# A second layer in f16 halves instead of fp32r, one attention chunk back to f16, more tiles and a new written order

## The chip, the cores and the metric

One NeuronCore of a Trainium2 chip runs the whole program. The metric is the device time of one execution in microseconds, taken as the median of several runs. Its compute engines are TensorE (PE in the profile: matmuls; PEld: the loading of their stationary operand), VectorE (DVE) and ScalarE (ACT). SyncE (SP) issues all data transfers here. GpSimd (POOL) only clears a few tiles at the start.

## The reference, cut to what matters

An attention with a complex decaying state is followed by a two-layer network. Batch is 4, heads 8, sequence 768, head width 48; the network is 384 to 2048 to 384 over 3072 rows.

```
scale = min(mag, 0.999) / (mag + 1e-6)          # mag = |a_re + i a_im|
for t in range(S):
    S_re, S_im = (a * S).re + k_t v_t^T, (a * S).im      # a = scaled a_re + i a_im
    y[t] = q_t @ S_re
x = y as rows of 384                             # 4 * 768 rows
h = x @ w_in
out = (h - tanh(h)) @ w_out
```

## The kernel before, in words

The sequence is cut into six chunks of 128 positions. A unit u is one chunk of one batch entry, so u runs from 0 to 23, chunk u // 4. A group g is two units, 256 rows of the network, and there are NG = 12 groups.

**The gates** (`gates_b` to `gates_e`, letters B, b, C, D, E in the written order) turn a_re and a_im of a group into decay factors and angles: logarithms, exponentials, an arctan, a cumulative sum over the 128 positions as a matmul with a triangle of ones (`cumsum`, L224 in fp32 for the first groups, L227 in f16 after them), sines. ScalarE must load a table of functions when it changes between logarithm, arctan or tanh, and sine.

**The products** (`products`, letter p) scale q and k of a unit with these factors (L395, L398: tile qkf) and bring them into transposed form, in fp32 through TensorE for the first chunk ("plain"), later split into a high and a low f16 part and transposed by a transfer that SP issues (L410, tiles qT and kT). The products of a unit also split v (tile vv, L421 and L422).

**The attention** (`attention`, letter a) forms the scores from kT and qT, masks them (tile af or a16), adds what the carried state z gives to q (L471), multiplies the masked scores with v (y, L478 in fp32, L481 in f16), writes the unit's rows as f16 halves x16, transposes them by a transfer into xT (L493), and updates the state z with k and v. A product of two split operands is three matmuls, high by high, high by low and low by high (`PASS`). For units below WIDE = 8, that is chunks 0 and 1, y and the state update take fp32 operands, without a split: one fp32 matmul per head, which the profile records as two. Units below PLAIN = 4 also have fp32 scores.

**The weights** come as 64-bit floats. `decode` (letters i and o for tile numbers of the first and second layer) loads a tile of 128 by 384 and builds the 32-bit value from the halves with three operations of VectorE (L187, L191, L192) and one of ScalarE (L110). Then ScalarE writes a high part and VectorE the low part. First-layer tiles become f16 pairs; second-layer tiles become fp32r pairs, a 4-byte format of TensorE. There are 16 tiles of each kind. The loaded tile is an io tile (three of them) or, for some, a borrowed mg tile; the scratch is a wtmp tile (three) or a borrowed mt tile, as the strings ROOM say.

**The network** works on a group at a time, in eight steps fp of two hidden tiles. `head` runs 18 f16 matmuls (L529) into a PSUM tile h (three of them), then tanh on ScalarE into an mt tile (two) and h - tanh(h) on VectorE over it. `split` writes the fp32r high part on ScalarE and the low part on VectorE into an mg tile (three). `tail` runs 12 matmuls of 384 columns (L554) into two PSUM tiles that collect all eight steps; it is written LAG = 4 steps behind the head. After step 7 ScalarE copies the sums out to an io tile and SP stores them.

**What sets the order.** START, FIRST, SECOND and CYCLE are lists written by hand: START is what comes ahead of the first group, FIRST and SECOND what is woven between the steps of groups 0 and 1, CYCLE that of all later ones. "8:a2" means: at place 8 (step 4, before its split) one more part of the attention of unit 2g + 2. On top of that each kind of operation has a priority offset (EARLY for groups 0 and 1, OFFSET later), by which the scheduler puts the instructions of each engine in order. Each engine and SP then run their queues in that order. So chunk 1, units 4 to 7, is worked on within groups 1 and 2.

**The guards.** Sums of squares and similar numbers of many tiles are collected in `stats`; `check_stats` compares them with limits and sets a flag. If the flag is set, a slow general version (`tile_general`) runs; it isn't set here. The check stands ahead of the last group's steps.

Of the kernel before, what the change touches and what calls it, by code (L numbers as in the profile page):

```python
# [84 lines left out]
def tile_fast(ctx: ExitStack, tc: tile.TileContext, flag, a_in, qkv_in, win_in, wout_in, sq_c, vec_c, lim_c, out):  # L85
# [84 lines left out]
    def decode(ft, kinds=(0, 1)):  # L170
        for kind in kinds:
            src = (win_in, wout_in)[kind]
            n = len(wi) + len(wo)
# [5 lines left out]
            SP("dec").dma_start(out=raw, in_=src[:, ft].bitcast(I32).rearrange("p (n two) -> p n two", two=2))
            if ROOM["wtmp"][n] == "1":  # L180
                tmp = sb.tile([P, 512], F32, name="mt", bufs=2)[:, :DM].bitcast(I32)
            else:
                tmp = sb.tile([P, DM], I32, name="wtmp", bufs=3)
# [248 lines left out]
    def attention(u):  # L432
# [3 lines left out]
        if g not in xTs:  # L436
            xTs[g] = sb.tile([P, 2, 2, KT, P], F16, name="xT", bufs=2)
# [392 lines left out]
```

## Time and profile before

| what | us |
|---|---|
| median of three runs | 596.84 |
| the three runs | 596.11, 596.84, 601.57 |
| the profiled execution | 599.23 |
| its span | 597.4 |
| TensorE matmuls busy | 532.2 |
| TensorE weight loads busy | 478.5 |
| VectorE busy | 469.1 |
| ScalarE busy | 465.2 |

The profile is of one execution, a little slower than the median. Its lines read: source line, engine, operation, the tile written and the tiles read, the shapes, and the count; then busy time, the mean of one in nanoseconds, and how long the engine idled just before, with what ended that. L100 is the line of a helper through which most operations are issued, so these are told apart by their tiles. A timeline line is the start, the length and the instructions, merged where they follow each other. Matmuls overlap, so a record is longer than the spacing of two of them. A wait "X <- Y" names the engine that idled and the operation whose end released it. The granted clock is the share of full speed that TensorE was given.

### The profile page before, as it was taken

To read this page: it belongs to the slowest core of one execution; us is meant where nothing else is said; L and a number is where in the kernel's file an instruction comes from. 1 tells how busy PE (TensorE), PEld (TensorE's weight loads), DVE (VectorE), ACT (ScalarE), POOL (GpSimd) and SP (SyncE) were. 2 spreads that over 40 slices of the span, in tenths; PEclk is the share of its full clock that TensorE was granted. 3 is DMA by queue.
4 is the path that set the end of the run, shared out by engine and by line. 5 is a ranking of instruction groups with operands and counts; after the bars stand their busy time and mean duration, and the time that the engine had idled before them with its cause. 6 is when DMAs were issued, how large, how long until landed. Compare 5 with 4: busy or idle time off the path is not lost.

```text
span 597.4 us, 12550 instructions
## 1 busy us (share of the span) xinstructions
PE 532.2 (89%) x4994; PEld 478.5 (80%) x4994; DVE 469.1 (79%) x790; ACT 465.2 (78%) x905; POOL 2.1 (0%) x8
## 2 busy tenths in 40 slices
PE   2464795988999999998999999999999999999995
PEld 0253694987998998997998998989989989999994
DVE  5887899678798498898898998988988988854330
ACT  7979697598897497888998998988989979553331
POOL 1000000000000000000000000000000000000000
PEclk9868798799999699999999999999999999999998
DMA  7738516317566287176275294593573652710001
GB/s 259 216 124 232 166 54 176 94 51 144 132 122 153 54 159 154 58 126 164 53 145 133 55 192 110 76 168 100 105 157 68 132 104 55 140 55 14 22 7 31
DMA packets 133901, 68.07 MB, mean 114 GB/s; under 512 B 119982, under 2 KB 123694, under 8 KB 133836
## 3 DMA queue, kind: packets, MB, share of 16 engines
q1 hardware_dynamic: 133836, 67.21, 49.7%
q8 instruction: 40, 0.66, 0.4%
q14 instruction: 25, 0.20, 0.1%
HBM read 36.73 MB, written 4.78 MB: 69 GB/s over the span
## 4 chain that ended last, share of the span: by engine, by line
PE 50%; ACT 26%; DVE 9%; DMA 8%; issue 4%; SPq 0%; ACTq 0%; DVEq 0%
PE o L554 18%; PE h L529 16%; PE att L100 10%; ACT a_raw L100 4%; ACT L100 4%; DMA kT<-k 3%; ACT mg L100 3%; DMA qT<-q 3%; ACT junk L100 3%; ACT mt L100 3%; PE att L478 2%; PE att L471 2%; ACT g_t L100 2%; PE att L227 2%; ACT q L100 2%
## 5 line engine op out<-in xcount | busy, mean ns | idle before, releaser
L554 PE MATMUL o<-wo,mg 128*128 128x384 f32 x1152 | 226.8, 345 | 2.7 <-ACT mg L100 2.3
L529 PE MATMUL h<-xT,wi 128*128 128x256 f16 x1728 | 210.0, 275 | 3.1 <-DMA xT<-x 3.0
L554 PEld LDWEIGHTS o<-wo,mg 128*128 128x128 f32 x1152 | 196.2, 189 | 4.9 <-ACT mg L100 2.9
L529 PEld LDWEIGHTS <-wi 128*128 128x128 f16 x1728 | 164.5, 99 | 34.2 <-issue 10.3
L100 DVE TENSOR_TENSOR mg<-mt,mg 128x512 fp32r<-128x512 f32 x96 | 65.8, 687 | 37.4 <-ACT mg L100 37.2
L100 DVE SCALAR_TENSOR_TENSOR mt<-h,mt 128x512 f32<-128x512 f32 x96 | 65.4, 687 | 27.2 <-ACT mt L100 26.6
L100 ACT ACTIVATE mt<-h 128x512 f32<-128x512 f32 x96 | 55.8, 589 | 38.6 <-PE h L529 27.7
L100 ACT ACTIVATE mg<-mt 128x512 fp32r<-128x512 f32 x96 | 59.8, 625 | 25.5 <-PE o L554 25.3
L100 ACT ACT_TABLE_LOAD x39 | 50.0, 1283 | 1.3 <-PEq L823 0.8
L100 PE MATMUL att<-qT,kT 96*128 96x128 f16 (+1 forms) x544 | 44.2, 235 | 3.7 <-DMA kT<-k 3.0
L100 ACT ACTIVATE a_raw<-a_raw 128x768 f32<-128x768 f32 (+2 forms) x49 | 39.0, 797 | 0.2 <-DVE a_raw L100 0.2
L398 DVE TENSOR_TENSOR qkf<-qkv_raw,g_trig 128x768 f32<-128x768 f32 x40 | 37.3, 950 | 0.0
L100 PEld LDWEIGHTS <-kT 96*128 96x128 f16 x480 | 29.0, 99 | 7.5 <-DMA kT<-k 3.9
L100 DVE SCALAR_TENSOR_TENSOR g_t<-g_t,a_raw 128x768 f32<-128x768 f32 (+1 forms) x26 | 23.1, 890 | 0.5 <-ACT a_raw L100 0.5
L100 PE MATMUL att<-sqc,qkf 128*96 128x128 f32 x32 | 6.6, 370 | 18.6 <-DVE qkf L398 18.6
L100 DVE TENSOR_TENSOR af<-att,sqc 128x512 f32<-128x512 f32 x32 | 21.9, 686 | 1.3 <-PE att L100 0.4
L100 ACT ACTIVATE a<-af 128x512 f16<-128x512 f32 x32 | 19.2, 626 | 4.0 <-DVE af L100 4.0
L100 DVE TENSOR_TENSOR a<-af,a 128x512 f16<-128x512 f32 x32 | 21.2, 682 | 1.0 <-ACT a L100 0.9
L100 ACT ACTIVATE g_trig<-g_t 128x768 f32<-128x768 f32 (+1 forms) x26 | 20.3, 786 | 1.8 <-DVE g_t L100 1.7
L100 PEld LDWEIGHTS att<-sqc,qkf 128*96 128x96 f32 x32 | 4.8, 169 | 20.7 <-DVE qkf L398 11.7
L117 DVE TENSOR_TENSOR q<-qkf,q 128x768 f16<-128x768 f32 x20 | 19.0, 952 | 2.2 <-ACT q L100 2.2
L100 ACT ACTIVATE q<-qkf 128x768 f16<-128x768 f32 x20 | 16.8, 842 | 4.0 <-DMA qT<-q 3.9
(102 smaller groups left out, 732.9 us busy)
## 6 DMA issues: line engine op xcount, KB each, us to landing
qkv_raw<-in_qkv SPq DMA_DIRECT2D x24, 576.0 KB
a_raw<-in_a SPq DMA_DIRECT2D x22, 384.0 KB
io<-in_wout SPq DMA_DIRECT2D x15, 384.0 KB
io<-in_win SPq DMA_DIRECT2D x14, 384.0 KB
out_dram<-io SPq DMA_DIRECT2D x24, 192.0 KB
a_raw<-in_a SPq DMA_DIRECT2D x4, 192.0 KB
mg<-in_win SPq DMA_DIRECT2D x2, 384.0 KB
mg<-in_wout SPq DMA_DIRECT2D x1, 384.0 KB
```

The costliest lines, as they stand in the source:

```text
L100: return f(*a, **k)
L117: by_name[ENGINE[which]](kind).tensor_tensor(**k)
L227: T("cum").matmul(c_ps[:, :HD], lhsT=tri, rhs=hl[:, bb, i], start=(i == 0), stop=(i == 1))
L398: V("prod").tensor_tensor(out=f, in0=x[:, :, None].broadcast_to([P, H, 2, D]), in1=tg[:, :, sl].rearrange("p r (h d) -> p h r d", d=D), op ...
L471: T("qu").matmul(u_ps[:, h * D:(h + 1) * D], lhsT=qT[0:K, qp * H + h], rhs=z16[0:K, zp, h * D:(h + 1) * D], start=(h == 0 and n == 0), sto ...
L478: T("y").matmul(y_ps[:, h * D:(h + 1) * D], lhsT=a16[h // 4][:, (h % 4) * P:(h % 4 + 1) * P], rhs=vv[0][:, h * D:(h + 1) * D], start=(h == ...
L529: T("h").matmul(h_ps[:, j].rearrange("p (two t) -> p two t", two=2), lhsT=wi[ft][:, wp, kt * P:(kt + 1) * P], rhs=xT[:, :, xp, kt, :], sta ...
L554: T("o").matmul(o_ps[tt][:, :DM], lhsT=gg[:, gp, j * 256 + tt * P:j * 256 + (tt + 1) * P], rhs=wo[ft][:, wp], start=(ft == 0 and n == 0), ...
```

## The change

- Both kinds of weight tile are f16 pairs, with the same scale. The split of h - tanh(h) goes to f16, with a factor 2 to the 15; the low part is made by a scalar_tensor_tensor instead of a tensor_tensor. The copy of the sums out takes the factors away again.
- WIDE goes from 8 to 4: in chunk 1 too, v, the masked scores and k are split to f16, and y and the state update are three f16 matmuls per head.
- Tiles (BUFS): io and wtmp 4 instead of 3 and without borrowing, mt 4 instead of 2, mg 5 instead of 3 (each half as large), qT 3 instead of 2; the others stay.
- New guards: the copy of the sums out of all groups but the last collects its sum ("o", 22 of them), and the last group squares its eight high parts ("g"). The check moves from ahead of the last group to behind its steps, before the last tails.
- The lists START, FIRST, SECOND and CYCLE and the priority offsets are new. The engines of all operations stay.

```diff
-WIDE = 8
-ROOM = {"io": "00000000000000000000110000010000", "wtmp": "11001011101001010000000000000000"}
+WIDE = 4
+BUFS = {"io": 4, "wtmp": 4, "mt": 4, "mg": 5, "qkf": 2, "xT": 2, "a16": 3, "af": 2, "xf": 1, "x16": 1, "qT": 3, "kT": 2, "vv": 2, "z16": 2}
 START = (
-    "o0 F0 o7 q0 F1 B1 b1 i1 p0 p0 q1 p1 i3 i0 p1 i5 p1 p0 o3 i2 a0 a0 o1 i6 i8 a1 i7 o4 a0 E1 a0 o5 a1 a1 i11 a1 o6 C1 i10 o2 D1 i4 a0 "
+    "q0 i3 F0 F1 i1 o7 p0 q1 B1 p1 i5 o3 i0 p0 p1 b1 p1 p0 a0 a0 o1 a1 a1 i7 E1 o4 a0 i8 a0 i6 i2 i10 i11 a1 o5 a1 C1 o2 i15 a0 o6 i4 D1 "
 ).split()
...
 CYCLE = tuple((int(i), x) for i, x in (y.split(":") for y in (
-    "0:p2 0:w0 1:p2 2:p3 2:p3 2:p2 5:C2 5:D2 5:a2 5:a2 6:p3 6:a3 7:a2 7:a2 8:a3 9:a3 10:B3 10:a2 10:a3 10:a3 11:E2 11:b3 12:w1 14:a2 "
+    "0:p2 1:p2 2:p3 3:p3 4:w0 4:p2 5:C2 5:p3 5:D2 5:a2 5:a2 6:a3 7:a2 7:a2 8:a3 9:a3 10:B3 10:a2 10:a3 10:a3 11:E2 11:b3 13:a2 15:w1 "
 ).split()))
...
-            if kind == 0:
-                t = wi[ft] = const.tile([P, 2, DM], F16, name=f"wi{ft}")
-            else:
-                t = wo[ft] = const.tile([P, 2, DM], F32R, name=f"wo{ft}")
+            t = const.tile([P, 2, DM], F16, name=f"w{kind}_{ft}")
+            (wi, wo)[kind][ft] = t
...
-        th = sb.tile([P, 512], F32, name="mt", bufs=2)
+        th = sb.tile([P, 512], F32, name="mt", bufs=BUFS["mt"])
...
-        gg = sb.tile([P, 2, 512], F32R, name="mg", bufs=3)
-        copy("ghi", "ghi", gg[:, 0], th)
-        combine("glo", "glo", out=gg[:, 1], in0=th, in1=gg[:, 0], op=ALU.subtract)
+        gg = sb.tile([P, 2, 512], F16, name="mg", bufs=BUFS["mg"])
+        copy("ghi", "ghi", gg[:, 0], th, 2.0 ** SG)
+        V("glo").scalar_tensor_tensor(out=gg[:, 1], in0=th, scalar=2.0 ** SG, in1=gg[:, 0], op0=ALU.mult, op1=ALU.subtract)
+        if g == NG - 1:
+            A("guard").activation(out=junk()[:, :512], in_=gg[:, 0], func=AF.Square, accum_out=stat("g"))
...
-                copy("out", "out", o_sb[:, tt], o_ps[tt][:, :DM])
+                A("out").activation(out=o_sb[:, tt], in_=o_ps[tt][:, :DM], func=AF.Copy, scale=2.0 ** -(SG + SW), **({"accum_out": stat("o")} if g < NG - 1 else {}))
...
-        if g == NG - 1:
-            check_stats()
...
+    check_stats()
     for x in pend:
         tail(*x)
```

Of the priority offsets, those of the later groups change so (a lower one lets others pass ahead): tanh from 700 to -2000, the masked scores (af) from 4000 to -300, the state's high part (zhi) from 2000 to 100, v's low part (vlo) from 0 to 1000, the transfers in (load) from 2000 to 400, the weights' (dechi, declo) from 30 and -300 to 100 and 200, mt from 200 to 400; a few others by less.

More of the change, by code (lines that the diff above doesn't have):

```diff
@@ L59 @@
-ENGINE = {"qhi": "A", "khi": "A", "qlo": "V", "klo": "V", "cos": "V", "sin": "V", "zhi": "A", "qux": "A", "zmul": "V", "out": "A", "xf0": "A", "tr": "A", "vd": "A", "lsb0": "V", "lsb1": "V", "base": "A", "dechi": "A", "declo": "V", "abs": "A", "thhi": "A", "t2hi": "A", "t2lo": "V", "xhi": "A", "xlo": "V", "vhi": "A", "ahi": "A", "alo": "V", "ghi": "A", "glo": "V", "nf": "A", "t1": "V"}
+OFFSET = {"gate": 2000, "gatep": 700, "prod": 0, "prodp": -100, "qkhi": -30, "vhi": -30, "vlo": 1000, "zhi": 100, "zlo": -300, "S": 30, "af": -300, "ahi": -30, "alo": -2000, "qu": 0, "y": 0, "xf": -30, "kv": 2000, "z": 100, "guard": -2000, "h": 0, "tanh": -2000, "mt": 400, "ghi": 2000, "glo": -30, "o": 0, "out": -100, "dec": -100, "dechi": 100, "declo": 200, "table": -30, "cum": 0, "load": 400}
@@ new lines @@
+EARLY = {"gate": 2000, "gatep": 100, "prod": 0, "prodp": 0, "qkhi": -30, "vhi": 0, "vlo": -2000, "zhi": 1000, "zlo": -300, "S": 100, "af": 1000, "ahi": -700, "alo": -30, "qu": 0, "y": 4000, "xf": 0, "kv": 700, "z": 200, "guard": -700, "h": 0, "tanh": 30, "mt": 400, "ghi": 100, "glo": 30, "o": 0, "out": 700, "dec": 0, "dechi": 1000, "declo": 4000, "table": -300, "cum": 0, "load": 0}
+ENGINE = {"qhi": "A", "khi": "A", "qlo": "V", "klo": "V", "cos": "V", "sin": "V", "zhi": "A", "qux": "A", "zmul": "V", "xf0": "A", "tr": "A", "vd": "A", "lsb0": "V", "lsb1": "V", "base": "A", "dechi": "A", "declo": "V", "abs": "A", "thhi": "A", "t2hi": "A", "t2lo": "V", "xhi": "A", "xlo": "V", "vhi": "A", "ahi": "A", "alo": "V", "ghi": "A", "glo": "V", "nf": "A", "t1": "V"}
@@ L172, in decode @@
             src = (win_in, wout_in)[kind]
-            n = len(wi) + len(wo)
-            if ROOM["io"][n] == "1":
-                raw = sb.tile([P, 2, 512], F32R, name="mg", bufs=3).rearrange("p two n -> p (two n)")[:, :2 * DM]
-            else:
-                raw = sb.tile([P, 2, DM], F32, name="io", bufs=3).rearrange("p two n -> p (two n)")
-            raw = raw.bitcast(I32).rearrange("p (n two) -> p n two", two=2)
+            raw = sb.tile([P, 2, DM], F32, name="io", bufs=BUFS["io"]).rearrange("p two n -> p (two n)").bitcast(I32).rearrange("p (n two) -> p n two", two=2)
             SP("dec").dma_start(out=raw, in_=src[:, ft].bitcast(I32).rearrange("p (n two) -> p n two", two=2))
[L180 to L183, printed above, removed]
+            tmp = sb.tile([P, DM], I32, name="wtmp", bufs=BUFS["wtmp"])
             lo, hi = raw[:, :, 0], raw[:, :, 1]
@@ L202, in weight_stats @@
         A("guard").activation(out=junk()[:, :DM], in_=wi[ft][:, 0], func=AF.Square, accum_out=stat("w"))
-        A("guard").activation(out=junk()[:, :DM], in_=wo[ft][:, 0], func=AF.Square, scale=2.0 ** 10, accum_out=stat("w"))
+        A("guard").activation(out=junk()[:, :DM], in_=wo[ft][:, 0], func=AF.Square, accum_out=stat("w"))
     gate = {}
@@ L395, in products @@
             V("prod").scalar_tensor_tensor(out=x, in0=vw(e), scalar=E_MAX, in1=x, op0=ALU.min, op1=ALU.mult)
-            f = kf if wide and i else sb.tile([P, H, 2, D], F32, name="qkf", bufs=2)
+            f = kf if wide and i else sb.tile([P, H, 2, D], F32, name="qkf", bufs=BUFS["qkf"])
             n = "qk"[i]
@@ L436, in attention @@
         if g not in xTs:
[L437 removed]
+            xTs[g] = sb.tile([P, 2, 2, KT, P], F16, name="xT", bufs=BUFS["xT"])
         xT = xTs[g]
@@ L441, in attention @@
         if c > 0:
-            z16 = sb.tile([P, 2, HD], F16, name="z16", bufs=2)
+            z16 = sb.tile([P, 2, HD], F16, name="z16", bufs=BUFS["z16"])
             zs = float(2.0 ** (SU - SZ))
@@ L460, in attention @@
                 continue
-            ah = sb.tile([P, 2, 512], F16, name="a16", bufs=3)
+            ah = sb.tile([P, 2, 512], F16, name="a16", bufs=BUFS["a16"])
             a16.append((ah, af))
@@ L487, in attention @@
         else:
-            xf = sb.tile([P, HD], F32, name="xf")
+            xf = sb.tile([P, HD], F32, name="xf", bufs=BUFS["xf"])
             copy("xf0", "xf", xf, y_ps[:, :HD], xs)
-        x16 = sb.tile([P, 2, HD], F16, name="x16")
+        x16 = sb.tile([P, 2, HD], F16, name="x16", bufs=BUFS["x16"])
         copy("xhi", "xf", x16[:, 0], xf)
```

37 lines of the change are left out of this document (18 added, 19 removed).

## The prediction

> **What bounds the kernel now.** First the page's busy times, then the busy times by stretch. I cut the span where TensorE starts the first-layer matmuls of a new group of 256 rows: the first at 64.25 us, the second at 128.42, the fourth at 219.92; 361.27 to 402.68 is one whole later group, and from 520.58 on no attention is left to prepare. The columns are the length, then PE, PEld, DVE, ACT and POOL busy (with instructions), granted clock, DMA share and GB/s.
>
> ```profile
> PE 532.2 (89%) x4994; PEld 478.5 (80%) x4994; DVE 469.1 (79%) x790; ACT 465.2 (78%) x905; POOL 2.1 (0%) x8
> ```
>
> ```profile
> 0.00:64.25 64.25, 27.95 (x137) 20.50 (x138) 49.28 (x104) 54.14 (x114) 2.08 (x8) 0.82 0.68 202
> 64.25:128.42 64.17, 54.99 (x373) 48.70 (x372) 53.29 (x104) 48.80 (x91) 0.00 (x0) 0.86 0.40 117
> 128.42:219.92 91.50, 87.73 (x780) 79.53 (x781) 71.32 (x111) 74.03 (x142) 0.00 (x0) 0.94 0.57 116
> 361.27:402.68 41.41, 40.50 (x441) 36.84 (x441) 37.30 (x61) 37.18 (x74) 0.00 (x0) 1.00 0.61 116
> 520.58:597.40 76.82, 69.41 (x592) 64.06 (x589) 28.45 (x46) 25.88 (x47) 0.00 (x0) 0.98 0.11 29
> ```
>
> The reader is to see four regimes. Up to 128.4 us TensorE waits for the others, which decode weights. In groups 1 and 2 (128.42 to 219.92) it is busy 87.7 of 91.5 us, partly at a lower clock. In the nine groups from 219.92 on it is the bound: 40.50 of 41.41 us, with VectorE and ScalarE close behind (37.30 and 37.18, 90%). At the end it runs alone. So a shorter TensorE instruction pays in full from 219.92 on, and only while the other two stay below it. The waits (total, times, longest) say what is late elsewhere:
>
> ```profile
> PE att L100 <- DVE qkf L398: 18.6, 3, 8.4
> PE att L227 <- ACT a_raw L100: 8.1, 8, 2.6
> ```
>
> **Second layer in f16 (term 1).** 1152 matmuls at L554 keep their count and their 384 columns. Their spacing is read from runs without a gap: the difference of a long and a short run of one kind. The same width in f16 is in the trace too, the cumulative sums of L227. Rows: start, length, what. The grouped lines and the counts by stretch follow.
>
> ```profile
> 163.75 0.49 PE L227 MATMUL att<-g_t,tri 128*128 128x384 f16 x2
> ...
> 462.10 0.82 PE L227 MATMUL att<-g_t,tri 128*128 128x384 f16 x4
> ...
> 575.15 2.33 PE L554 MATMUL o<-wo,mg 128*128 128x384 f32 x12
> ...
> 579.22 10.65 PE L554 MATMUL o<-wo,mg 128*128 128x384 f32 x60
> ```
>
> ```profile
> L554 PE MATMUL o<-wo,mg 128*128 128x384 f32 x1152 | 226.8, 345 | 2.7 <-ACT mg L100 2.3 <-DVE mg L100 0.4
> ...
> L227 PE MATMUL att<-g_t,tri 128*128 128x384 f16 x40 | 8.5, 328 | 0.0
> ```
>
> ```profile
> 128.42:219.92 91.50, 32.23 (x156) 27.29 (x156) 0.94 0.57 116
> 219.92:597.40 377.48, 178.37 (x913) 154.55 (x912) 1.00 0.47 98
> ```
>
> Now (10.65 - 2.33) / 48 = 173.3 ns; f16 (0.82 - 0.49) / 2 = 165 ns. The saving is 8.3 ns each: 913 x 8.3 = 7.6 us after 219.92, and 1.3 us for the 156 in groups 1 and 2, which belongs to term 3. Bounds: nothing, if the 173 ns come from the tile and not from the type; and 17 ns by the two means (345 - 328), 15.5 us. I take **-7.6**, since a spacing counts and not a length.
>
> The Trainium skill speaks against this term: "FP8 and Floating Point Precision", section TensorE Precision Notes, lists four passes for true FP32 and has reduced-precision FP32 merely read 4 bytes and cut them. By that, both forms are one pass over the same columns and term 1 is 0. The 173.3 against 165 ns above disagree, on two rounded rows.
>
> What feeds these matmuls does not change in price by any row: the high part stays a ScalarE copy (f32 to f16 is among the forms below at 626 ns), the low part becomes a scalar_tensor_tensor in place of a tensor_tensor, and the factors ride along. By the rows under term 3 the one form costs 682/512 = 1.33 ns a column and the other 550/384 = 1.43; were it 0.1 ns dearer, that is 0.4 us of VectorE a group (8 x 512 columns), beside TensorE's 40. I take 0.
>
> **More tiles for tanh and its split (term 2).** In each late group TensorE stops once, before the cumulative sum of L227, for ScalarE:
>
> ```profile
> 395.79 2.14 PE L529 MATMUL h<-xT,wi 128*128 128x256 f16 x18
> ...
> 398.62 0.60 ACT L100 ACTIVATE mt<-h 128x512 f32<-128x512 f32 x1 [1.36 <-DVE mg L100]
> ...
> 402.68 0.48 PE L227 MATMUL att<-a_raw,tri 128*128 128x384 f16 x2 [0.90 <-ACT a_raw L100]
> ```
>
> The tanh at 398.62 waits for one of two mt tiles, which the low-part operation frees. Its matmuls ended at 397.93, so 0.7 us of the 1.36 are the tile's. The arctan that TensorE waits for stands behind it in ScalarE's queue. With four mt tiles the 0.90 us stop can shrink to 0.2; what is late next is the table load and the copy of the angle. Eight stops of 0.7 are 5.6 us; at best all 8.1 us of the wait above go. I take half, **-3**, since tanh's priority also falls (from 700 to -2000); the bad end of that is worked out as a rival.
>
> The Trainium skill, "Perfetto Trace Analysis", section Optimization Strategy, reads a repeated bubble on the engine that should be full as a possible lack of tile space. By that rule the whole 8.1 us would go with the new tiles; the rows above give the tile only 0.7 of the 0.9 us.
>
> **Chunk 1 back to f16 (term 3).** Units 4 to 7 (attention of chunk 1, run in groups 1 and 2) get 24 f16 matmuls for y and 24 for the state update, where 16 records each stand now (8 fp32 matmuls are 16 records). Spacing is the start of the next row less the start:
>
> ```profile
> 149.06 1.96 PE L478 MATMUL att<-qkv_raw,a 128*128 128x48 f32 x16
> 150.86 0.82 PE L529 MATMUL h<-xT,wi 128*128 128x256 f16 x6
> ...
> 164.74 1.48 PE L100 MATMUL att<-af,vv 128*96 128x48 f32 x16
> 166.05 1.25 PE L529 MATMUL h<-xT,wi 128*128 128x256 f16 x10
> ...
> 449.57 0.78 PE L471 MATMUL att<-z,qT 96*128 96x48 f16 x24
> 450.19 0.56 PE L481 MATMUL att<-vv,a 128*128 128x48 f16 x16
> ```
>
> y 1.80 to 0.62, state 1.31 to 0.62 (24 matmuls of the same 48 columns): 1.87 us per unit, 7.5 us of TensorE for four. Against it stands work on the other two engines:
>
> ```profile
> L100 DVE TENSOR_TENSOR a<-af,a 128x512 f16<-128x512 f32 x32 | 21.2, 682 | 1.0 <-ACT a L100 0.9
> ...
> L100 ACT ACTIVATE a<-af 128x512 f16<-128x512 f32 x32 | 19.2, 626 | 4.0 <-DVE af L100 4.0
> ...
> L421 DVE SCALAR_TENSOR_TENSOR vv<-qkv_raw,vv 128x384 f16<-128x384 f32 x16 | 8.8, 550 | 1.0 <-ACT vv L100 1.0
> ...
> L100 ACT ACTIVATE vv<-qkv_raw 128x384 f16<-128x384 f32 x16 | 8.3, 521 | 0.1
> ...
> L422 DVE TENSOR_SCALAR vv<-vv,vec 128x768 f16<-128x768 f16 x16 | 6.6, 412 | 0.1
> ...
> L110 ACT ACTIVATE af<-qkv_raw,vec 128x384 f32<-128x384 f32 x6 | 3.5, 603 | 0.2 <-PE att L100 0.2
> ```
>
> VectorE: 2 x 682 + 550 + 412 = 2.33 us per unit, 9.3 in all. ScalarE: 2 x 626 + 521 - 603 = 1.17, 4.7 in all. In the 91.5 us VectorE goes from 71.3 to 80.6 and ScalarE from 74.0 to 78.7, TensorE from 87.7 to 78.9. These groups then hold the same work as a late one, which takes 41.41 - 0.8 (96 x 8.3 ns) = 40.6 us: two take 81.2, 10.3 less than now. The loads of the raw q, k, v also move, from behind the y matmuls to the end of the products, four of them, each earlier on SP's queue; SP waits for y there now:
>
> ```profile
> SPq L152 <- PE att L478: 13.8, 4, 6.5
> ```
>
> Bounds: -10.3, and +9.3 if all of VectorE's new work falls on the path. These groups still start late and cold after group 0, so I take half the good end, **-5**.
>
> **New order and tiles at the start (term 4).** Up to the first group the lists hold the same 19 weight tiles, six product steps and nine attention steps; only their order differs, and the decode's scratch is four io and four wtmp tiles instead of three and three with loans from mg and mt. The transposes of the first q and k wait for VectorE:
>
> ```profile
> 35.44 1.91 PE L100 MATMUL att<-sqc,qkf 128*96 128x128 f32 x8 [8.42 <-DVE qkf L398]
> ...
> SPq L179 <- DVE wtmp L192: 35.0, 12, 9.3
> ```
>
> While TensorE waits there, VectorE does decode work. The new list puts q0, p0 and p1 ahead of most tiles, and a fourth io tile loosens SP's 35 us of waits for a free one, behind which the attention's transfers queue. But VectorE and ScalarE are busy 102.6 and 102.9 of the first 128.4 us, and that work stays. Bounds: all 18.6 us of waits for qkf above, or one wait more of 8.4. Nearest to nothing: **-2**.
>
> **Guards and the end (0).** 22 output copies get a read of the accumulator (0.2 us each, as the row below), 0.4 us of ScalarE a group, beside TensorE's 40. Eight squares of 512 columns in the last group, at most 0.63 + 0.20 us each, lie where ScalarE is busy 25.9 of 76.8 us. The check comes behind the last of them instead of ahead of the last group; its load of limits then stands on SP ahead of nothing but the last outputs, and only the flag waits for it.
>
> ```profile
> L100 ACT ACTIVATION_READ_ACCUMULATOR junk<-xf 128x1 f32 x24 | 4.7, 194 | 0.0
> ```
>
> ```profile
> 590.02 0.15 DVE L100 TENSOR_SCALAR flag<-att 1x1 int32<-1x1 f32 x1 [5.00 <-PE att L100]
> ```
>
> ```profile
> L778 SPq EVENT_SEMAPHORE  x8: 17/17/17, 595.5 to 596.0; - x8
> L778 SPq COMPARE_BRANCH  x1: 53/53/53, 591.6 to 591.6; - x1
> ```
>
> The branch on the flag is done at 591.6; the end waits for the outputs to land, to 595.5. A flag up to 3.9 us later costs nothing; without that cover the last square and its read (0.8 us) would be added.
>
> **Sum.** The profiled execution took 599.23 us (span 597.4 and 1.8 around it): 599.2 - 7.6 - 3 - 5 - 2 = 581.6. The median shown, 596.84, is 2.4 lower, so **579.2**.
>
> **The rivals.**
> (a) The second layer does not get faster (term 1 at its bound of nothing): 579.2 + 7.6 = **586.8**. For it: the f16 spacing rests on short runs of one fixed weight tile. Against it: the two spacings differ by 8 ns. The Trainium skill's rule quoted under term 1 gives this result too.
> (b) VectorE and ScalarE become the bound in the late groups. They are at 90% with 41.41 us; at 40.6 ScalarE with its reads stands at 37.6, 93%, in strict order on each engine. If the period stays, terms 1 and 2 go but for the last stretch (592 records, some 190 of them second layer, 1.6 us): 579.2 + 6.0 + 3 = 588.2, and half of term 3 with it, **590.7**. Against it: the stops of TensorE in a late group are 0.9 us.
> (c) Slower: the splits of chunk 1 stand between the scores and y. In each of units 4 to 7 TensorE would wait for two high and two low parts, 2 x (0.626 + 0.682) = 2.6 us, and lose its clock as it does now after its wait for a transposed k:
>
> ```profile
> 193.00:206.00 13.00, 13.00 (x122) 11.94 (x118) 6.32 (x12) 4.15 (x10) 0.00 (x0) 0.61 0.27 76
> ```
>
> 13 us at 0.61 lose 5.1. Four times 7.7 is 30.8, less the 7.5 that the matmuls save: +23.3 in place of -5, 579.2 + 28.3 = **607.5**. It decides from 5.0 us lost per unit on: 4 x 5.0 - 7.5 is +12.5 in place of -5, as much as the forecast gains. Against it: from 219.92 on the same splits leave the clock at 1.00.
> (d) The order at the start gives most of the waits for qkf, 14 instead of 2: **567.2**.
>
> **How the numbers follow.** Forecast 0.50 (own range 571 to 587), (a) 0.09, (b) 0.17, (c) 0.12, (d) 0.12. A measurement of this kernel tells about 1%, 6 us, from no change: faster means below 590.9, slower above 602.8. Forecast, (a), (d) and a third of (b): 0.77 faster; the rest of (b) 0.11 the same; (c) 0.12 slower. The range runs from (d) to where (c) begins, 565 to 602.
>
> **What would show it.** Right: runs of 60 second-layer matmuls near 9.9 us; late groups of 40 to 40.6 us with TensorE stopped under 0.5 us; groups 1 and 2 together near 86; the first first-layer matmul within 3 us of 64. Wrong: 173 ns kept (a); late groups still at 41.4 with ScalarE or VectorE at the waits' head (b); a clock below 0.9 in the y matmuls of chunk 1 (c); first layer starting before 55 (d).

## The result and the profile after

| | before | after |
|---|---|---|
| median, us (four runs each, same chip) | 596.53 | 575.27 |
| range of the runs | 596.11 to 601.57 | 574.78 to 577.2 |
| the profiled execution | 599.23 | 575.09 |
| its span | 597.4 | 573.3 |

The ratio is 0.9631 [0.9575, 0.9687]: faster by 3.7%. The forecast was 579.2.

First the busy times on the page of the kernel after, then its busy times by stretch, cut at the same places as before: where TensorE starts the first-layer matmuls of group 0, 1, 3 and 11. The columns are the length, PE, PEld, DVE, ACT and POOL busy (with instructions), granted clock, DMA share and GB/s.

```profile
PE 502.8 (88%) x5058; PEld 385.8 (67%) x5058; DVE 475.2 (83%) x806; ACT 474.1 (83%) x951; POOL 2.3 (0%) x8
```

```profile
0.00:68.25 68.25, 26.81 (x128) 18.49 (x129) 55.33 (x119) 56.66 (x121) 2.26 (x8) 0.91 0.71 212
68.25:116.44 48.19, 46.50 (x369) 37.86 (x370) 45.96 (x90) 42.01 (x80) 0.00 (x0) 0.95 0.44 124
116.44:209.18 92.74, 79.55 (x863) 59.50 (x861) 80.97 (x131) 83.75 (x161) 0.00 (x0) 0.98 0.58 113
209.18:527.27 318.09, 310.51 (x3411) 241.75 (x3412) 279.76 (x450) 273.96 (x554) 0.00 (x0) 0.99 0.53 114
527.27:573.30 46.03, 39.41 (x292) 28.17 (x289) 13.20 (x21) 17.68 (x39) 0.00 (x0) 0.98 0.06 20
```

The same stretch of late groups in the kernel before:

```profile
219.92:548.86 328.94, 320.43 (x3418) 291.61 (x3417) 282.61 (x455) 275.31 (x539) 0.00 (x0) 1.00 0.53 110
```

The difference of the spans, 24.1 us, by stretch:

| stretch | before | after | difference | forecast |
|---|---|---|---|---|
| ahead of group 0 | 64.2 | 68.3 | +4.0 | |
| group 0 | 64.2 | 48.2 | -16.0 | -2 with the line above |
| groups 1 and 2 | 91.5 | 92.7 | +1.2 | -5 |
| groups 3 to 10 | 328.9 | 318.1 | -10.8 | |
| group 11 and the end | 48.5 | 46.0 | -2.5 | -10.6 with the line above |

The reader is to see that half the gain comes from the place for which 2 us were forecast. Up to the start of group 1, VectorE does nearly the same work, 55.33 + 45.96 = 101.3 us against 49.28 + 53.29 = 102.6; what shrank is the time in which it idles, from 25.9 us of 128.4 to 15.2 of 116.4. In groups 3 to 10 TensorE is busy 9.9 us less and idles 7.6 us instead of 8.5.

The second-layer matmuls of the kernel after, in the timeline (start, length, what) and in the groups:

```profile
552.73 2.11 PE L548 MATMUL o<-w,mg 128*128 128x384 f16 x12
...
556.64 9.91 PE L548 MATMUL o<-w,mg 128*128 128x384 f16 x60
```

```profile
L548 PE MATMUL o<-w,mg 128*128 128x384 f16 x1152 | 204.3, 326 | 1.7 <-ACT mg L102 1.0
...
L548 PEld LDWEIGHTS <-mg 128*128 128x128 f16 x1152 | 111.3, 98 | 66.0 <-ACT mg L102 1.2
```

The spacing is (9.91 - 2.11) / 48 = 162.5 ns, where it was 173.3: 10.8 ns less per matmul. The waits (total, times, longest) of TensorE in the kernel after:

```profile
PE att L102 <- DVE qkf L390: 15.8, 2, 11.9
PE h L521 <- DMA xT<-x: 10.9, 3, 7.0
...
PE att L219 <- ACT a_raw L102: 9.0, 9, 2.6
```

The stop before the cumulative sum is still there, 9.0 us in 9 where it was 8.1 in 8. A wait for xT, the transposed rows of the attention, has taken second place; its longest, 7.0 us, ends at 68.25 with the first matmul of group 0, where the kernel before waited 1.28 us.

### The profile page after: what moved, and what is told of

Its sections match the earlier page's. It is cut to its first block, busy times and chain, and to the rows that moved or that the text cites. A ratio compares the mean times of both kernels' runs of the same rounds, so it can differ in the third digit from the quotient of the medians.

```text
span 573.3 us, 12669 instructions
## 1 busy us (share of the span) xinstructions
PE 502.8 (88%) x5058; PEld 385.8 (67%) x5058; DVE 475.2 (83%) x806; ACT 474.1 (83%) x951; POOL 2.3 (0%) x8
## 4 chain that ended last, share of the span: by engine, by line
PE 34%; ACT 27%; DVE 22%; DMA 9%; issue 7%; SPq 1%; ACTq 0%; DVEq 0%
PE h L521 11%; PE o L548 10%; PE att L102 8%; ACT L102 5%; ACT a_raw L102 5%; DMA qT<-q 4%; DVE qkf L390 3%; DMA kT<-k 3%; DVE g_t L102 3%; ACT mg L102 3%; DVE qkv_raw L387 2%; DVE q L119 2%; ACT mt L102 2%; ACT g_t L102 2%; DVE mg L102 2%
## 5 line engine op out<-in xcount | busy, mean ns | idle before, releaser
L521 PE MATMUL h<-xT,w 128*128 128x256 f16 x1728 | 209.8, 275 | 13.5 <-DMA xT<-x 10.9
L548 PE MATMUL o<-w,mg 128*128 128x384 f16 x1152 | 204.3, 326 | 1.7 <-ACT mg L102 1.0
L521 PEld LDWEIGHTS <-w 128*128 128x128 f16 x1728 | 168.6, 99 | 43.9 <-DMA xT<-x 8.6
L548 PEld LDWEIGHTS <-mg 128*128 128x128 f16 x1152 | 111.3, 98 | 66.0 <-ACT mg L102 1.2
L102 DVE SCALAR_TENSOR_TENSOR mg<-mt,mg 128x512 f16<-128x512 f32 x96 | 65.0, 687 | 17.4 <-ACT mg L102 16.5
L102 ACT ACTIVATE mg<-mt 128x512 f16<-128x512 f32 x96 | 59.1, 626 | 16.3 <-DVE mt L102 16.1
L390 DVE TENSOR_TENSOR qkf<-qkv_raw,g_trig 128x768 f32<-128x768 f32 x44 | 41.1, 952 | 0.0
L102 DVE TENSOR_TENSOR a<-af,a 128x512 f16<-128x512 f32 x40 | 27.2, 686 | 7.8 <-ACT a L102 7.7
L102 DVE TENSOR_TENSOR af<-att,sqc 128x512 f32<-128x512 f32 x40 | 27.3, 687 | 5.4 <-PE att L102 4.3
L102 ACT ACTIVATE a<-af 128x512 f16<-128x512 f32 x40 | 24.8, 623 | 3.7 <-DVE af L102 3.7
L102 ACT ACTIVATE w<-wtmp 128x384 f16<-128x384 f32 x32 | 16.1, 518 | 8.4 <-DVE wtmp L186 8.4
L102 PE MATMUL att<-sqc,qkf 128*96 128x128 f32 x32 | 7.0, 386 | 16.2 <-DVE qkf L390 15.8
```

The source lines that it names most:

```text
L102: return f(*a, **k)
L390: V("prod").tensor_tensor(out=f, in0=x[:, :, None].broadcast_to([P, H, 2, D]), in1=tg[:, :, sl].rearrange("p r (h d) -> p h r d", d=D), op ...
L521: T("h").matmul(h_ps[:, j].rearrange("p (two t) -> p two t", two=2), lhsT=wi[ft][:, wp, kt * P:(kt + 1) * P], rhs=xT[:, :, xp, kt, :], sta ...
L548: T("o").matmul(o_ps[tt][:, :DM], lhsT=gg[:, gp, j * 256 + tt * P:j * 256 + (tt + 1) * P], rhs=wo[ft][:, wp], start=(ft == 0 and n == 0), ...
```

## The experiments

Each ratio is to the kernel before on the same chip. There its median was 596.53 us beside the kernel after, and 599.07, 599.39 or 600.6 beside the kernels below, so kernels are compared by their ratios and not by their medians. The first two kernels below start from the kernel before, all others from the kernel after. The stretches are of one profiled execution each, in us. In the six kernels with START, the offsets and the decode's tiles as changed, the stretch ahead of group 0 ranges from 68.3 to 70.0, so a difference of 2 us there says little.

| kernel | ratio | ahead | group 0 | 1 and 2 | 3 to 10 | rest |
|---|---|---|---|---|---|---|
| before | 1 | 64.2 | 64.2 | 91.5 | 328.9 | 48.5 |
| after | 0.9631 | 68.3 | 48.2 | 92.7 | 318.1 | 46.0 |
| second layer f16 only | 0.9871 | 65.8 | 64.3 | 86.0 | 325.7 | 46.7 |
| the same with mt 4, mg 5 | 0.9858 | 65.0 | 61.6 | 95.8 | 318.5 | 46.4 |
| after, chunk 1 in fp32 | 0.9638 | 68.6 | 48.3 | 92.2 | 319.2 | 46.6 |
| after, old lists and offsets | 0.9939 | 69.2 | 58.7 | 96.7 | 323.1 | 46.0 |
| after, old lists | 0.9873 | 69.8 | 57.5 | 93.5 | 323.6 | 46.2 |
| after, old offsets | 0.9829 | 66.0 | 61.5 | 92.3 | 319.3 | 46.1 |
| after, mt 2 | 0.9756 | 70.5 | 48.0 | 95.4 | 321.6 | 46.0 |
| after, mg 3 | 0.9702 | 69.2 | 48.8 | 92.6 | 321.6 | 45.8 |
| after, qT 2 | 0.9580 | 69.5 | 48.6 | 92.8 | 318.1 | 46.1 |
| after, mt 2 and mg 3 | 1.0156 | 69.0 | 49.0 | 94.2 | 349.9 | 46.0 |
| after, mt 2, mg 3, qT 2 | 1.0216 | 70.0 | 49.4 | 92.8 | 346.4 | 46.1 |
| after, io 5, wtmp 6 | 0.9745 | 73.9 | 53.3 | 90.1 | 316.4 | 46.1 |

### The second layer in f16 alone

The kernel before with f16 weights and f16 halves of the second layer; nothing else. The mg tile keeps its size and its count, and the halves lie in its first part.

```diff
-                t = wo[ft] = const.tile([P, 2, DM], F32R, name=f"wo{ft}")
+                t = wo[ft] = const.tile([P, 2, DM], F16, name=f"wo{ft}")
...
-        gg = sb.tile([P, 2, 512], F32R, name="mg", bufs=3)
-        copy("ghi", "ghi", gg[:, 0], th)
-        combine("glo", "glo", out=gg[:, 1], in0=th, in1=gg[:, 0], op=ALU.subtract)
+        gg = sb.tile([P, 2, 512], F32, name="mg", bufs=3).rearrange("p two n -> p (two n)").bitcast(F16)[:, :1024].rearrange("p (two n) -> p two n", two=2)
+        copy("ghi", "ghi", gg[:, 0], th, 2.0 ** SG)
+        V("glo").scalar_tensor_tensor(out=gg[:, 1], in0=th, scalar=2.0 ** SG, in1=gg[:, 0], op0=ALU.mult, op1=ALU.subtract)
```

> The kernel before with nothing changed but the second layer: its weight tiles and the split of h - tanh(h) are f16 pairs, the factors as in the changed kernel; tiles, lists, priorities, chunk 1 and the place of the check stay. Theory 1, the term is the matmul spacing alone (173.3 to 162.5 ns in the two profiles, 10.8 ns) and pays in full from group 3 on: 913 x 10.8 = 9.9 us and some 1 to 2 us from groups 1 and 2, so 585 to 587 us, late groups near 40.3 us. Theory 2, ScalarE and VectorE hold the late groups at 41.4 us unless the order and the tiles change too: 593 to 596 us.

Measured: 591.01 us, 0.9871 [0.9791, 0.995], between the two expectations. Its timeline, waits and busy times by stretch:

```profile
567.27 2.11 PE L555 MATMUL o<-wo,mg 128*128 128x384 f16 x12
...
571.18 9.91 PE L555 MATMUL o<-wo,mg 128*128 128x384 f16 x60
```

```profile
PE att L228 <- ACT a_raw L101: 14.6, 8, 3.2
...
ACT mt L101 <- DVE mg L101: 10.6, 9, 1.6
```

```profile
216.11:541.81 325.70, 311.25 (x3417) 242.59 (x3416) 282.72 (x456) 275.40 (x539) 0.00 (x0) 0.99 0.54 111
```

The type alone makes the spacing 162.5 ns. In groups 3 to 10, 8 x 96 x 10.8 ns = 8.3 us were to be had and 3.2 came. TensorE's busy time fell from 320.4 to 311.3, but its idle time rose from 8.5 to 14.5, almost all of it in one wait, from 8.1 to 14.6: for the arctan on ScalarE, which stands behind a tanh that waits for an mt tile. The tanh's own wait is no longer than in the kernel before, 10.6 us in 9 in both; TensorE comes sooner. Groups 1 and 2 fall from 91.5 to 86.0 us, more than the 1.7 us that the spacing gives there (156 x 10.8 ns); the granted clock in them is 1.00 in this execution and 0.94 in that of the kernel before.

### The same with more tiles for tanh and its split

```diff
-        th = sb.tile([P, 512], F32, name="mt", bufs=2)
+        th = sb.tile([P, 512], F32, name="mt", bufs=4)
...
-        gg = sb.tile([P, 2, 512], F32, name="mg", bufs=3).rearrange("p two n -> p (two n)").bitcast(F16)[:, :1024].rearrange("p (two n) -> p two n", two=2)
+        gg = sb.tile([P, 2, 512], F32, name="mg", bufs=5).rearrange("p two n -> p (two n)").bitcast(F16)[:, :1024].rearrange("p (two n) -> p two n", two=2)
```

> The kernel before with the f16 second layer and mt 4, mg 5 (the tiles that are lent to the decode grow in number too); lists, offsets, chunk 1, io and wtmp as before. The f16 second layer alone took 591.01 us, late groups 41.1. Theory 1, the tiles let the late groups use the shorter matmuls under any order: late groups near 40.3, 582 to 586. Theory 2, the tiles help only with the new order: 589 to 592.

Measured: 590.0 us, 0.9858 [0.9814, 0.9902]. Busy times by stretch, groups 1 and 2 and then groups 3 to 10, and the wait:

```profile
126.61:222.45 95.84, 87.64 (x809) 67.92 (x806) 76.28 (x120) 80.49 (x153) 0.00 (x0) 0.98 0.50 110
222.45:540.95 318.50, 309.87 (x3418) 241.25 (x3416) 281.60 (x455) 274.52 (x540) 0.00 (x0) 1.00 0.55 114
```

```profile
PE att L228 <- ACT a_raw L101: 7.9, 8, 2.4
```

So the late groups did what the first expectation said and the time as a whole what the second said. In groups 3 to 10 the tiles give 7.2 us, and the stretch is as long as in the kernel after. There f16 and tiles are enough for the whole gain: old lists, old offsets and chunk 1 in fp32 stand in this kernel. But groups 1 and 2 take 9.8 us more than in the kernel without the tiles, so the time as a whole stays. A part of that is work that changed its place: TensorE has 809 records there against 781, and 346 against 372 in group 0. Up to the start of group 3 the loss is 222.45 - 216.11 = 6.3 us. What loses it wasn't settled. The clock in group 0 is 0.74 against 0.86, and the decode, which borrows mt and mg tiles in this kernel, has more of them too.

### Chunk 1 in fp32 again

```diff
-WIDE = 4
+WIDE = 8
```

> The changed kernel with chunk 1 put back to fp32 y and state products (WIDE 8), all else as changed. Theory 1, the split of chunk 1 gave back on VectorE and ScalarE what it saved on TensorE: within 3 us of the changed kernel, 572 to 578, with groups 1 and 2 again 92 to 93 us together. Theory 2, as predicted it saves 5 us: 580. Theory 3, its 9.3 us of VectorE lie on the path of group 1, which became 7.8 us longer: 566 to 569.

Measured: 576.74 us, 0.9638 [0.9565, 0.9712], the same as the kernel after. Groups 1 and 2:

```profile
116.86:209.07 92.21, 85.09 (x798) 66.51 (x796) 72.94 (x113) 79.42 (x151) 0.00 (x0) 1.00 0.53 114
```

The f16 form takes 5.5 us of TensorE away (79.55 against 85.09) and gives 8.0 to VectorE and 4.3 to ScalarE; the stretch is 92.7 against 92.2. This part of the change gains and loses nothing that these runs can tell, as the first expectation had it.

### Old lists and old offsets, together and each alone

Three kernels: lists and offsets of the kernel before, the lists alone, the offsets alone, with all other parts of the change. One line of each edit, of the list of the later groups and of the offsets of groups 0 and 1:

```diff
-    "0:p2 1:p2 2:p3 3:p3 4:w0 4:p2 5:C2 5:p3 5:D2 5:a2 5:a2 6:a3 7:a2 7:a2 8:a3 9:a3 10:B3 10:a2 10:a3 10:a3 11:E2 11:b3 13:a2 15:w1 "
+    "0:p2 0:w0 1:p2 2:p3 2:p3 2:p2 5:C2 5:D2 5:a2 5:a2 6:p3 6:a3 7:a2 7:a2 8:a3 9:a3 10:B3 10:a2 10:a3 10:a3 11:E2 11:b3 12:w1 14:a2 "
```

```diff
-EARLY = {"gate": 2000, "gatep": 100, "prod": 0, "prodp": 0, "qkhi": -30, "vhi": 0, "vlo": -2000, "zhi": 1000, "zlo": -300, "S": 100, "af": 1000, "ahi": -700, "alo": -30, "qu": 0, "y": 4000, "xf": 0, "kv": 700, "z": 200, "guard": -700, "h": 0, "tanh": 30, "mt": 400, "ghi": 100, "glo": 30, "o": 0, "out": 700, "dec": 0, "dechi": 1000, "declo": 4000, "table": -300, "cum": 0, "load": 0}
+EARLY = {"gate": 2000, "gatep": 4000, "prod": 0, "prodp": -2000, "qkhi": -30, "vhi": 0, "vlo": -2000, "zhi": -30, "zlo": -300, "S": 400, "af": 4000, "ahi": -700, "alo": 100, "qu": 0, "y": 0, "xf": 0, "kv": 700, "z": 200, "guard": -700, "h": 0, "tanh": 2000, "mt": 200, "ghi": 100, "glo": 30, "o": 0, "out": 700, "dec": 0, "dechi": 30, "declo": 4000, "table": -300, "cum": 0, "load": 0}
```

> The changed kernel with the old written lists and the old priority offsets, all else (f16, chunk 1, tiles, place of the check) as changed. Theory 1, the 12 us gained up to the start of group 1 come from the order: 586 to 589, with the first group again near 64 us long. Theory 2, they come from the tiles of the decode and of tanh, and the order is worth little: 575 to 579.

> The changed kernel with the old written lists alone; the priority offsets, tiles, f16 and chunk 1 as changed. With both lists and offsets old it took 594.98 us, 20 more than the changed kernel, of which 10.5 us in the first group, 4 in groups 1 and 2 and 5 in the late groups. Theory 1, the lists set the first groups and the offsets the late ones: first group near 58 us, late groups near 39.8, 587 to 591. Theory 2, the offsets carry it, the lists almost nothing: 575 to 580. Theory 3, lists and offsets only work as a pair: over 592.

> The changed kernel with the old priority offsets alone; lists, tiles, f16 and chunk 1 as changed. Old lists and offsets together took 594.98 us, old lists alone 591.3. Theory 1, the offsets matter little (3.7 us between those two): 576 to 580, late groups 39.8 to 40.3. Theory 2, the new lists need the new offsets: over 586.

Measured: both old 594.98 us, 0.9939 [0.9902, 0.9976]; lists old 591.3, 0.9873 [0.9818, 0.9928]; offsets old 589.57, 0.9829 [0.9776, 0.9883]. With both old, the time came out above both expectations. With the lists old it is just outside the first, 587 to 591: group 0 is as expected there, but the late groups take 40.5 us and not 39.8. With the offsets old it is in the second, over 586. Against both old, the new offsets alone give 0.7 percentage points, with intervals that overlap, and the new lists alone 1.1; together they give 3.1. Group 0 shows it most plainly: 58.7 us with neither, 57.5 with the offsets, 61.5 with the lists, 48.2 with both. The first two stretches with both old, and then with the new lists and the old offsets:

```profile
0.00:69.21 69.21, 27.87 (x128) 20.07 (x129) 53.12 (x113) 56.03 (x118) 2.09 (x8) 0.80 0.71 204
69.21:127.91 58.70, 51.01 (x380) 39.31 (x380) 49.53 (x96) 44.15 (x83) 0.00 (x0) 0.94 0.38 108
```

```profile
0.00:66.02 66.02, 27.03 (x128) 18.71 (x129) 53.10 (x113) 54.46 (x115) 1.94 (x8) 0.93 0.71 214
66.02:127.48 61.46, 54.01 (x381) 40.78 (x380) 50.69 (x98) 47.05 (x91) 0.00 (x0) 0.86 0.35 104
```

VectorE is busy 102.7 of 127.9 us with both old, 103.8 of 127.5 with the offsets old and 101.3 of 116.4 in the kernel after. It is its idle time that the two parts of the order close between them, from 25.3 and 23.7 to 15.2 us. The clock in group 0 doesn't account for it: it is 0.95 in the kernel after and 0.86 with the offsets old, but 0.94 with both old, where group 0 takes 58.7 us. The wait for qkf at the start, on which the prediction's case of a large gain rested, is 15.8 us with the offsets old and in the kernel after, so it is not what changed between these two.

One thing is left open: with old lists and old offsets this kernel takes 323.1 us for groups 3 to 10, where f16 with the tiles, also with the old order, took 318.5. TensorE's stops before the cumulative sum in these groups are 11.5 us against 7.7, most of the 4.6. The two differ in chunk 1, qT, the tiles of the decode and the size of mg, the new guards and the place of the check, and none of the runs tells which it is.

### Fewer tiles for tanh, its split and the transposed q

Five kernels with tile counts as in the kernel before, for one, two or all three of mt, mg and qT. The edit with all three:

```diff
-BUFS = {"io": 4, "wtmp": 4, "mt": 4, "mg": 5, "qkf": 2, "xT": 2, "a16": 3, "af": 2, "xf": 1, "x16": 1, "qT": 3, "kT": 2, "vv": 2, "z16": 2}
+BUFS = {"io": 4, "wtmp": 4, "mt": 2, "mg": 3, "qkf": 2, "xT": 2, "a16": 3, "af": 2, "xf": 1, "x16": 1, "qT": 2, "kT": 2, "vv": 2, "z16": 2}
```

> The changed kernel with the old numbers of tiles for tanh, its split and the transposed q (mt 2, mg 3, qT 2), all else as changed. Theory 1, the stop of TensorE before the cumulative sum is set by ScalarE's chain and not by the tiles, as nine stops of 9.0 us in all remain with the new tiles: 575 to 577. Theory 2, the tiles carry the predicted 3 us or more by letting ScalarE and VectorE run ahead in the late groups: 578 to 583.

Then each alone, with the other counts as after the change. The kernel with mt 2 has one difference more than the text below says: the priority offset that is also called mt, of the operation that forms h - tanh(h), is 200 instead of 400 there, in both lists of offsets. So its time isn't that of the tile count alone.

> The changed kernel with two tiles for tanh (mt 2) alone; mg 5 and qT 3 as changed. With mt 2, mg 3 and qT 2 it took 611.83 us and late groups of 44.6. Theory 1, the tanh tile is what holds ScalarE's queue (a tanh that can't start blocks the arctan and the splits behind it): 600 to 612, late groups 43 to 45. Theory 2, the split's tile is: 575 to 582.

> The changed kernel with three tiles for the split (mg 3) alone; mt 4 and qT 3 as changed. Theory 1, the tanh tile is the one that matters: 575 to 582. Theory 2, the split's tile, which the tails four steps later free, matters as much or more, since at LAG 4 three tiles make the split wait for the tail: 595 to 612 with ScalarE waiting for the second layer's matmuls.

> The changed kernel with two tiles for the transposed q (qT 2) alone. With mt 2, mg 3 and qT 2 together it took 611.83 us, with mt 2 alone 583.29, with mg 3 alone 580.80: 36.6 more against 8.0 and 5.5. In the slow one ScalarE waited 23.0 us for loads of raw q, k, v. Theory 1, the third qT tile carries the rest: a transposing transfer that waits for a tile holds SP's queue, and the loads behind it come late: 592 to 605, with ScalarE's waits for these loads near 20 us. Theory 2, it is worth nothing alone and the shortages multiply: 574 to 578.

And mt 2 with mg 3:

> The changed kernel with mt 2 and mg 3, qT 3 as changed. Theory 1, the third qT tile was most of the 36.6 us, the other two add up: 586 to 592, no long wait for raw loads. Theory 2, tanh's and the split's tiles together cost far more than each alone: 600 to 612.

Measured: all three 611.83 us, 1.0216 [1.0137, 1.0295]; mt 2 583.29, 0.9756 [0.9705, 0.9807]; mg 3 580.8, 0.9702 [0.966, 0.9745]; qT 2 575.46, 0.958 [0.952, 0.964]; mt 2 with mg 3 609.82, 1.0156 [1.0101, 1.0211]. All three together miss both expectations by far, 611.83 us where 578 to 583 was the larger. The third qT tile gains nothing that these runs can tell. The kernel with mt 2 and the changed offset loses 1.3 percentage points, mg 3 loses 0.7 with intervals that overlap, and both tiles together lose 5.3. That the tiles stand in for each other would fit these numbers; it isn't shown, since mt 2 was not run without the changed offset. What happens when both are short, in the waits, the stretch of groups 3 to 10 and the timeline of one late group of that kernel:

```profile
ACT rawsq L102 <- DMA qkv_raw<-in_qkv: 24.8, 8, 4.3
PE att L219 <- ACT a_raw L102: 24.7, 9, 3.7
```

```profile
212.22:562.08 349.86, 322.06 (x3409) 248.90 (x3410) 281.14 (x449) 273.51 (x551) 0.00 (x0) 0.96 0.49 104
```

```profile
404.13 0.32 ACT L102 ACTIVATE rawsq<-qkv_raw 128x144 f32<-128x144 f32 x1 [4.06 <-DMA qkv_raw<-in_qkv]
404.36 0.58 ACT L102 ACTIVATE mt<-h 128x512 f32<-128x512 f32 x1
404.83 0.83 ACT L102 ACTIVATE a_raw<-a_raw 128x768 f32<-128x768 f32 x1
...
407.51 0.83 ACT L102 ACTIVATE a_raw<-a_raw 128x768 f16<-128x768 f32 x1
...
408.39 0.49 PE L219 MATMUL att<-a_raw,tri 128*128 128x384 f16 x2 [3.23 <-ACT a_raw L102]
```

And the same place in the kernel after:

```profile
422.55 0.83 ACT L102 ACTIVATE a_raw<-a_raw 128x768 f32<-128x768 f32 x1
...
425.23 0.83 ACT L102 ACTIVATE a_raw<-a_raw 128x768 f16<-128x768 f32 x1
425.96 0.31 ACT L102 ACTIVATE rawsq<-qkv_raw 128x144 f32<-128x144 f32 x1
426.11 0.48 PE L219 MATMUL att<-a_raw,tri 128*128 128x384 f16 x2 [0.40 <-ACT a_raw L102]
```

With few tiles, ScalarE's queue has a guard, the square of a raw q, k and v tile, ahead of the tanh and the arctan. The guard takes 0.3 us but waits 4.06 for its load, and TensorE's cumulative sum waits 3.23 behind it. With the tiles the guard stands behind the arctan's copy and no one waits for it. Lists and offsets are the same in these two kernels, so the tile counts also set the order in which the scheduler writes each engine's queue. The guard stands ahead of the arctan in six of the seven places of this kernel's groups 3 to 10, in none of the kernel after or with mg 3 alone, and in one with mt 2. TensorE's waits of this kernel in groups 3 to 10 alone:

```profile
PE att L219 <- ACT a_raw L102: 22.0, 7, 3.7
PE h L521 <- DVE mt L102: 5.7, 6, 1.0
```

Of the 31.8 us that these groups lose, the stop before the cumulative sum is 22.0 - 7.4 = 14.6, the wait of the first layer for VectorE's h - tanh(h), which the kernel after doesn't have there, 5.7, and TensorE's longer busy time, at a clock of 0.96 instead of 0.99, another 11.6.

### More tiles for the decode

```diff
-BUFS = {"io": 4, "wtmp": 4, "mt": 4, "mg": 5, "qkf": 2, "xT": 2, "a16": 3, "af": 2, "xf": 1, "x16": 1, "qT": 3, "kT": 2, "vv": 2, "z16": 2}
+BUFS = {"io": 5, "wtmp": 6, "mt": 4, "mg": 5, "qkf": 2, "xT": 2, "a16": 3, "af": 2, "xf": 1, "x16": 1, "qT": 3, "kT": 2, "vv": 2, "z16": 2}
```

> The changed kernel with more scratch for the decode (io 5, wtmp 6). The first first-layer matmul stands at 68.3 us in the changed kernel and at 64.2 to 65.8 in the three with the old scratch (three io and three wtmp with loans). Theory 1, the decode lacks scratch now, and more of it brings the start back to 65: 572 to 573, faster than the changed kernel. Theory 2, the start is set by VectorE's and ScalarE's work and its order: 575 to 576, start at 68.

Measured: 584.57 us, 0.9745 [0.9693, 0.9798], slower than the kernel after and above both expectations. Its first two stretches and its longest wait:

```profile
0.00:73.91 73.91, 32.23 (x145) 23.03 (x146) 61.10 (x130) 59.18 (x127) 2.11 (x8) 0.68 0.72 216
73.91:127.24 53.33, 47.93 (x365) 37.31 (x363) 42.59 (x81) 41.97 (x80) 0.00 (x0) 0.94 0.28 84
```

```profile
PE att L102 <- DVE qkf L390: 25.6, 3, 11.6
```

With more scratch the decode runs ahead of the attention: VectorE does 61.1 us of work before the first group instead of 55.3, and TensorE waits 25.6 us for qkf instead of 15.8. No kernel tried here beats the kernel after by more than its interval.

## Why the prediction was right in the sum and wrong in the parts

The forecast was 581.6 us on the profiled execution's own time; it took 575.1. The parts missed by more than the sum: the start and group 0 by -10.0, groups 1 and 2 by +6.2, all later by -2.7. That the sum came within 6.5 us is in part luck, since a miss of +6.2 stands against two of -12.7 together. Of the signs named for being right, one came: runs of 60 matmuls take 9.91 us. The late groups are shorter than said, 39.8 us, but TensorE still stops about 1 us in each (9.0 in 9) and not under 0.5, groups 1 and 2 take 92.7 us and not 86, and the first layer starts at 68.25.

**Second layer (term 1): mechanism right, size too small.** The saving is 10.8 ns a matmul, not 8.3, so 913 of them give 9.9 us instead of 7.6. The price was read from the cumulative sums, two matmuls of difference in rows of hundredths; the long run gives 162.5, not 165. Rival (a) is out: the type alone made the spacing shorter. So is, here, the price that the prediction drew from "FP8 and Floating Point Precision" of the Trainium skill, section TensorE Precision Notes, the same for both forms: they take 173.3 and 162.5 ns.

The step named the condition ("only while the other two stay below it") and put nothing for it into the sum: these 9.9 us need room elsewhere. By itself f16 gave 3.2 of the 8.3 us in groups 3 to 10; the rest turned into a longer stop. This is rival (b) in part: the period fell from 41.1 us (328.9 / 8) to 40.7, not to the 40.1 that f16 alone could give. With the tiles it is 39.8.

**Tiles (term 2): size about right by luck, mechanism wrong.** "With four mt tiles the 0.90 us stop can shrink to 0.2" did not come: the wait for the arctan is 9.0 us in 9 against 8.1 in 8. The one late group shown above stops 0.40 us, but the sum of the waits counts. After the 9.9 us of term 1, the later part's 13.3 us leave 3.4 for all else, against the 3 forecast. But f16 alone with and without tiles differs by 7.2 us: the tiles' work is that the shorter matmuls count, and not that an old stop goes. The Trainium skill's page "Perfetto Trace Analysis", section Optimization Strategy, says that repeated bubbles can mean a lack of tile space. As the prediction read it, all 8.1 us would have gone. Tiles were short for the faster engine: without them the bubble is 14.6 us, with them 7.9, as long as before. No run gives the tiles to the kernel with fp32r matmuls, so what they do there stays open.

**Chunk 1 (term 3): wrong.** The step that failed is "These groups then hold the same work as a late one". On TensorE they nearly do. But they hold 81.0 us of VectorE's work and 83.8 of ScalarE's, where two of the groups 3 to 10 hold 69.9 and 68.5. The prediction's own sum had VectorE at 80.6 us, which leaves it hardly any slack in the 81.2 it gave the two groups. They took 92.7 us, and with chunk 1 in fp32 92.2. The trade of TensorE's 5.5 us for VectorE's 8.0 is near what was worked out (7.5 and 9.3); it moves nothing. TensorE idles 13.2 of 92.7 us, and VectorE and ScalarE are at 87 and 90%. The second layer in f16 alone had the two groups at 86.0 us already; which later part takes that back isn't known. The two groups and the matmul that starts group 2, in the kernel after:

```profile
116.44:168.14 51.70, 41.02 (x442) 30.12 (x440) 43.97 (x71) 47.75 (x91) 0.00 (x0) 1.00 0.62 111
168.14:209.18 41.04, 38.53 (x422) 29.37 (x421) 37.00 (x62) 35.99 (x72) 0.00 (x0) 0.96 0.54 116
```

```profile
168.14 7.72 PE L521 MATMUL h<-xT,w 128*128 128x256 f16 x54 [2.89 <-DMA xT<-x]
```

Group 2 is near a late one, 41.0 us. Group 1 takes 51.7: ScalarE has 47.8 us of work in it, and the group ends with TensorE waiting for the rows of units 4 and 5. Part of what group 0 gives comes back here. Group 1 starts 12 us sooner than in the kernel before, but the transfers that transpose the rows of units 4 and 5 start only 7.2 and 5.9 us sooner (149.05 and 163.59 us against 156.29 and 169.50). The chain that ends in that matmul (start, length, what) holds two transposing transfers of k and one of the rows:

```profile
134.50 4.81 DMA kT<-k
...
143.87 6.99 DMA kT<-k
...
163.59 4.51 DMA xT<-x
```

What would shorten it was not tried. Rival (c), a clock lost to the splits, is out: the clock is 0.98.

**The start (term 4): the direction right, the size not.** "VectorE and ScalarE are busy 102.6 and 102.9 of the first 128.4 us, and that work stays": the work did stay, but VectorE was idle a fifth of the time, 25.9 us, and 15.2 are left; with the old lists and offsets it is 25.3. I had bounded the gain by the wait for qkf; the wait went from 18.6 only to 15.8 us. The gain comes instead in group 0, 16.0 us less 4.0 lost ahead of it, where nothing in the list of waits was long. Group 0 was the place to look: it took 64.2 us, and its busiest engine, TensorE at a clock of 0.86, had 55.0 us of work. Now it takes 48.2 with 46.5. In the kernel with the rest of the change, the new order accounts for nearly all of it: group 1 starts at 127.9 us with old lists and offsets, at 116.4 with the new ones, and at 128.4 in the kernel before. Rival (d) had the gain, and by another way than it said.

**Guards and the end (nothing): the runs agree.** Group 11 and the end take 46.0 us; with f16 and tiles, but the old guards and the old place of the check, they take 46.4. In the kernel after the flag is written at 566.72 and the branch on it done at 568.3, while the last outputs land at 571.4 to 571.9:

```profile
566.72 0.14 DVE L102 TENSOR_SCALAR flag<-att 1x1 int32<-1x1 f32 x1 [5.77 <-PE att L102]
```

```profile
L771 SPq EVENT_SEMAPHORE  x8: 17/17/17, 571.4 to 571.9; - x8
L771 SPq COMPARE_BRANCH  x1: 53/53/53, 568.3 to 568.3; - x1
```

The cover shrank from 3.9 to 3.1 us.

## What to carry to other kernels

A shorter instruction on the engine that bounds a stage pays only as far as the others, here at 90%, have tiles to run ahead: f16 alone gave 3.2 of 8.3 us, with tiles all of it. Look for a gain where a stage takes longer than its busiest engine works (64 us against 55), even if its list of waits is short, and test lists and priorities as one thing: alone, new lists and new offsets gave 1.1 and 0.7 percentage points, together 3.1. Look at the order of the queues after a change of tile counts, since it can change with them. More scratch wasn't better by itself here: with it, decode work that was ready took the place of work that was needed.

## What the runs showed of the hardware

A 384-column matmul with fp32r operands is spaced 173.3 ns apart and its f16 twin 162.5; the record of its weight load is 189 ns against 98. TensorE's load time fell from 478.5 to 385.8 us, by 92.7 us, most of it in the second layer's loads, but by their spacing its matmuls got only 1152 x 10.8 ns = 12.4 us shorter: most of the load had been hidden beside matmuls.

```profile
L554 PEld LDWEIGHTS o<-wo,mg 128*128 128x128 f32 x1152 | 196.2, 189 | 4.9 <-ACT mg L100 2.9 <-DVE mg L100 0.8
```

The row is of the kernel before; 196.2 - 111.3 = 84.9 us of the 92.7 are these loads.
